# Norms of q computed one channel per partition and spread over the partitions by a diagonal product; first transposes ahead of the norms; four groups beside the first softmax

## The chip, the cores and the metric

The kernel runs on one core of one Trainium2 chip. The metric is device time in microseconds (us) of one execution; lower is better. Engines are named as the profile names them: PE is TensorE (matrix products; PEld is the loading of its weights), DVE is VectorE, ACT is ScalarE, POOL is GpSimd, SP is SyncE, which here only issues loads. Each engine works through its own instructions in order; they wait for each other on semaphores.

## What is computed

Attention over channels, with its product fused into a gated convolution. q, k, v are (4, 6336, 256), all in fp32:

```python
qn = q / (np.linalg.norm(q, axis=1, keepdims=True) + 1e-06)
kn = k / (np.linalg.norm(k, axis=1, keepdims=True) + 1e-06)
s = kn.transpose(0, 2, 1) @ qn / tau          # 256 x 256 for each of 4 batches
s = s - s.max(-1, keepdims=True)
a = np.exp(s)
a /= a.sum(-1, keepdims=True) + 1e-09
x = v @ a                                     # (4, 6336, 256)
# causal depthwise convolution over 5 rows, a gate, and two 256 x 256 products
gate = 1 / (1 + np.exp(-sum(conv_w[k] * shifted(x, k) for k in range(5))))
out = (gate * (x @ w_val)) @ w_out
```

The kernel does not normalise q and k ahead of the product. It sums k'q over the 6336 rows, sums the squares of every column of q and k beside it, and divides the 256 x 256 result once.

## The kernel before

**Groups.** A batch's rows are cut into 49 blocks of 128 rows and a rest of 64, and the blocks into 17 *groups*: the first has one block and the rest, the other 16 have three blocks. `load_group` loads a group of q and k (SP's queue). `score_group` squares it on ACT (`sq`, L209; the first block of a batch straight into the sums, L205), adds the squares on DVE (`acc_ps`, L214) and POOL (`acc`, L214), and returns the products that add k'q into the PSUM tile `s_ps` (L226). A block is multiplied either as it is (`raw`, one plain fp32 product for each half of k's channels) or split: ACT rounds it to fp32r (`hi`, L192), POOL subtracts to get the remainder (`lo`, L193), and three fp32r products stand for one. Which, is in one line: batch 0 multiplies most blocks raw, batch 1 its first LEAD groups, all else is split.

```python
nw, nv = (GROUP, 1 if g else 2) if b == 1 and g < LEAD else (0, 2)   # nw blocks raw, nv added on DVE
```

**Softmax.** `softmax(b)` is a generator that is advanced one stage by each `tick()`: `acc_all`, the sum of the two sums of squares (DVE L240), and a copy of `s_ps` to SBUF (ACT L242), which frees `s_ps` for the next batch; the norms (PE L245, L247) into a PSUM bank `n_ps`; Sqrt (ACT L252); on DVE the added epsilon (L256), two reciprocals (L257, L258), the scores scaled by both norms (L263) and their row minimum (L265); Exp (ACT L268); the sum's reciprocal and the scaled matrix `a` (L272, L275); `w`, its split into hi and lo (L278, L279); its transposes (PE L285, ACT `at` L289); and its product with w_val (PE L294, split by L298 and L299). So `x = v a` and the value product both read v alone, with two weights. `s_ps` and `acc_ps` exist once; the other PSUM tiles named here share four banks (`tag="bank"`), of which the norms hold one until L272.

In L245 the squares of q are summed over the partitions by a 128 x 128 matrix of ones, so that every partition gets all 256 norms of q along its row; the norms of k come out one channel per partition (L247), which is how the rows of the scores need them.

**Steps.** The rows of v are cut into 13 *steps* of 508 rows for each batch, 52 in all. For each, `transpose_v` (PE L335, ACT L336 `v_hi`, DVE L337 `v_lo`), `conv` (12 products L345 into `x_ps`, ACT L359, 8 DVE operations L361), `sigmoid` (ACT L367), `value` (12 products L345 into `val_ps`, DVE L374), `split_g` (ACT L387, POOL L388) and `finish` (24 products L404 into `o_ps`, ACT L414, stores from ACT's queue).

**Order.** The program starts with the 17 groups of batch 0, then a stretch written out by hand in which batch 1's first LEAD groups stand beside the softmax of batch 0, and then a loop over the 52 steps, in which the remaining groups are spread:

```python
due = NG + LEAD + -(-(total - NG - LEAD) * (n + 1) // (last + 1))
turns = min(due, total) - (issued - len(ready))
```

with NG = 17, total = 68 and last = 35. `turns` groups are multiplied in step n, the first near its start and the second, where there is one, near its end; their rounding, squares and subtraction are issued one group ahead. The four softmaxes' stages are advanced by the ticks of the steps that follow a batch's last group. A scheduler then orders each engine's instructions by its own estimate of times, with three means to steer it: `tc.high_priority()`, program order, and `behind(...)`, which keeps what is issued in it behind the marked instruction of an engine (`marks["PE"]`, `marks["ACT"]`).

Of the kernel before, what the change touches and what calls it, by code (L numbers as in the profile page):

```python
# [8 lines left out]
F32 = mybir.dt.float32  # L9
# [3 lines left out]
AF = mybir.ActivationFunctionType  # L13
# [3 lines left out]

P = 128
GROUP = 3
LEAD = 5  # L20
PREFETCH = 4
VLEAD = 2
SIDE = 11
# [5 lines left out]
def kernel(  # L29
# [136 lines left out]
    def score_group(b, g):  # L166
# [49 lines left out]
        def mms(np_, j):  # L216
            r = slice(0, np_)
            stop = g == NG - 1 and np_ == parts[-1][0] and j == parts[-1][1] + parts[-1][2] - 1
            for h in range(NH):
                hs = slice(h * P, (h + 1) * P)  # L220
                if j < nw:
                    ops = [(raw[r, j, 1, hs], raw[r, j, 0, :])]
                else:
                    ops = [(hi[r, j, 1, x, hs], hi[r, j, 0, y, :]) for x, y in ((0, 0), (0, 1), (1, 0))]
                for n_, (lhs, rhs) in enumerate(ops):
                    nc.tensor.matmul(st["s"][:, h, :], lhs, rhs, start=False,  # L226
                                     stop=stop and h == NH - 1 and n_ == len(ops) - 1)

        def clear():

# [5 lines left out]
    def softmax(b):  # L236
# [2 lines left out]
        acc = soft_p.tile([P, 2, C], F32, name="acc_all")  # L239
        nc.vector.tensor_tensor(acc, st["acc"], st["side"], ALU.add)  # L240
        s = soft_p.tile([P, NH, C], F32, name="s")
        nc.scalar.copy(s, st["s"])  # L242
        yield
        n_ps = ps.tile([P, 512], F32, name="o_ps", tag="bank")
        nc.tensor.matmul(n_ps[:, 0:C], ones, acc[:, 0, :], start=True, stop=True)  # L245
        for h in range(NH):
            marks["PE"] = nc.tensor.matmul(n_ps[:, C + h:C + h + 1], acc[:, 1, h * P:(h + 1) * P], ones[:, 0:1],  # L247
                                           start=True, stop=True)
        yield

        r, rk, z = n_ps[:, 0:C], n_ps[:, C:C + NH], n_ps[:, C + NH:C + 2 * NH]
        marks["ACT"] = nc.scalar.activation(n_ps[:, 0:C + NH], n_ps[:, 0:C + NH], AF.Sqrt)  # L252
        if b == 0:
            marks["ACT"] = tc.keep_in_program_order(nc.scalar.activation(dummy, dummy, AF.Exp))
        yield
        nc.vector.tensor_scalar(n_ps[:, 0:C + NH], n_ps[:, 0:C + NH], 1e-6, None, ALU.add)  # L256
        nc.vector.reciprocal(rk, rk)  # L257
        nc.vector.reciprocal(r, r)  # L258
        nk = soft_p.tile([P, NH], F32, name="nk")
        nc.vector.tensor_scalar(nk, rk, rtau, -1.0, ALU.mult, ALU.mult)  # L260

        for h in range(NH):
            nc.vector.scalar_tensor_tensor(s[:, h, :], s[:, h, :], nk[:, h:h + 1], r, ALU.mult, ALU.mult)  # L263
        m = soft_p.tile([P, NH], F32, name="m")
        nc.vector.tensor_reduce(m, s, axis=AX.X, op=ALU.min)  # L265
        yield
        for h in range(NH):
            marks["ACT"] = nc.scalar.activation(s[:, h, :], s[:, h, :], AF.Exp, scale=-1.0, bias=m[:, h:h + 1], accum_out=z[:, h:h + 1])  # L268
# [57 lines left out]
    def transpose_v(b, i, h):  # L326
# [5 lines left out]
        tp = ps.tile([P, 512], F32, name="t_ps", tag="bank")  # L332
        for j in range(-(-w // P)):
            np_ = min(P, w - j * P)
            nc.tensor.transpose(tp[:, j * P:j * P + np_], src[0:np_, j, h * P:(h + 1) * P], ident[0:np_, 0:np_])  # L335
        nc.scalar.copy(th[:, h, 0:w], tp[:, 0:w])  # L336
        nc.vector.tensor_tensor(tl[:, h, 0:w], tp[:, 0:w], th[:, h, 0:w].bitcast(F32), ALU.subtract)  # L337

# [114 lines left out]
    def run_group():  # L453
        if not ready:
            split_group()
        if not ready:
            return
        b, g, products = ready.pop(0)
        for f in products:
            f()  # L460
        if g == NG - 1:
            stages.append(softmax(b))
            if b:
                tick()
# [30 lines left out]
        for _ in gen:  # L495
            pass
    prep.clear()
    run_group()
    tick()
    tick()  # L500
    tick()
    with behind("PE", "ACT"):
        run_group()
        for h in range(NH):
            transpose_v(*step(0), h)
    tick()
    tick()
    with behind("ACT"):
# [1 line left out]
    tick()  # L510
    tick()
    tick()
    with behind("ACT"):
        for n in range(3, LEAD):
            run_group()
    for h in range(NH):
        conv(*step(0), h)
    while stages:
# [77 lines left out]
```

## Time and profile before

| | |
|---|---|
| time, median of 3 runs | 656.65 us (656.63 to 656.83) |
| the profiled execution's own time | 658.18 us |
| its span, first to last instruction | 656.3 us |
| PE busy | 637.8 us, 97% |
| DVE, ACT, POOL busy | 80%, 71%, 55% |
| TensorE's granted clock, mean | 0.996 |

The profile is of one execution. Busy time of PE is counted with modelled ends, so the time between the starts of two products says more of a product's price than its own length. Where an instruction waited, its row ends in brackets: the idle time of its engine just before it and what ended that.

### The profile page before, as it was taken

What the parts mean: (1) busy time and instruction counts of PE and PEld (TensorE: products, weight loads), DVE (VectorE), ACT (ScalarE), POOL (GpSimd) and SP (SyncE); (2) the same over time, 40 slices, a digit from 0 to 9 for tenths busy, and PEclk for the clock granted to TensorE, in tenths of its full rate; (3) what the DMA queues carried; (4) which work ended last, traced back from release to release, by engine and by line L of the source; (5) the groups of instructions that cost most, each with busy time, mean ns of one, the idle gap of its engine ahead of it and who ended that gap; (6) DMA issues with size and microseconds to landing.
All of it is one profiled execution on the core that took longest, in us unless ns stands there. A gap on an engine that the chain in (4) does not pass through costs nothing.

```text
span 656.3 us, 10656 instructions
## 1 busy us (share of the span) xinstructions
PE 637.8 (97%) x4008; PEld 571.1 (87%) x4008; DVE 523.0 (80%) x832; ACT 466.1 (71%) x607; POOL 360.8 (55%) x173
## 2 busy tenths in 40 slices
PE   7989999999999999999998999999999999999996
PEld 5868799989979999999997998998999798888886
DVE  3898689787878688778788688778778888888894
ACT  4565978867888768668698687767777756655564
POOL 2442796965837769659565497766763222312220
PEclk9999999999999999999999999999999999999999
DMA  8999874555635565545564365563222343443213
GB/s 268 322 328 337 267 225 152 161 166 165 179 103 176 188 195 176 173 132 170 175 184 121 109 217 158 189 185 104 65 78 71 118 126 95 121 129 104 65 50 100
DMA packets 107875, 105.75 MB, mean 161 GB/s; under 512 B 5744, under 2 KB 107312, under 8 KB 107824
## 3 DMA queue, kind: packets, MB, share of 16 engines
q1 hardware_dynamic: 81520, 79.24, 39.0%
q10 hardware_dynamic: 26304, 25.84, 13.9%
q8 instruction: 31, 0.51, 0.3%
q14 instruction: 20, 0.16, 0.1%
HBM read 79.11 MB, written 25.95 MB: 160 GB/s over the span
## 4 chain that ended last, share of the span: by engine, by line
PE 85%; ACT 5%; DVE 4%; POOL 2%; DMA 2%; issue 1%; SPq 1%; ACTq 0%; POOLq 0%
PE o_ps L404 20%; PE x_ps L345 20%; PE val_ps L345 19%; PE s_ps L226 18%; PE t_ps L335 6%; POOL hi L193 1%; ACT sq L209 1%; PE o_ps L294 1%; DMA raw<-in_k_dram 1%; DVE acc_ps L214 1%; ACT hi L192 1%; DVE gate L361 1%; DMA v_raw<-in_v_dram 1%; DVE gate L374 1%; ACT gate L367 0%
## 5 line engine op out<-in xcount | busy, mean ns | idle before, releaser
L361 DVE SCALAR_TENSOR_TENSOR gate<-x_ps,wa,gate 128x508 f32<-128x508 f32 (+1 forms) x416 | 275.4, 716 | 15.7 <-ACT gate L359 14.6
L193 POOL TENSOR_TENSOR hi<-raw,hi 128x1536 fp32r<-128x1536 f32 (+2 forms) x54 | 167.8, 3110 | 94.5 <-ACT hi L192 94.5
L388 POOL TENSOR_TENSOR g_lo<-gate,g_hi 128x1016 fp32r<-128x1016 f32 (+1 forms) x50 | 116.6, 2332 | 145.2 <-ACT g_hi L387 130.6
L214 DVE TENSOR_TENSOR acc_ps<-acc_ps,sq 128x512 f32<-128x512 f32 (+1 forms) x134 | 93.4, 697 | 74.8 <-ACT sq L209 71.6
L345 PE MATMUL x_ps<-v_hi,w 128*128 128x512 f32 (+1 forms) x416 | 139.1, 394 | 0.0
L345 PE MATMUL val_ps<-v_hi,w 128*128 128x508 f32 (+1 forms) x416 | 133.9, 383 | 0.8 <-ACT o_sb L414 0.7
L226 PE MATMUL s_ps<-hi 128*128 128x256 f32 (+1 forms) x852 | 121.1, 287 | 7.4 <-ACT hi L192 4.0
L226 PEld LDWEIGHTS s_ps<-hi 128*128 128x128 f32 (+1 forms) x852 | 110.7, 190 | 13.9 <-ACT hi L192 5.5
L404 PE MATMUL o_ps<-wo_hi,g_hi 128*128 128x256 f32 x400 | 113.2, 283 | 1.7 <-ACT g_hi L383 1.5
L414 ACT COPY o_sb<-o_ps 128x512 f32<-128x512 f32 x99 | 58.2, 589 | 79.1 <-PE o_ps L404 77.9
L404 PE MATMUL o_ps<-wo_lo,g_hi 128*128 128x256 f32 x400 | 112.1, 280 | 0.0
L404 PE MATMUL o_ps<-wo_hi,g_lo 128*128 128x256 f32 x400 | 111.7, 280 | 0.0
L209 ACT ACTIVATE sq<-raw 128x1536 f32<-128x1536 f32 (+3 forms) x69 | 96.0, 1393 | 16.5 <-DVE acc_ps L214 7.9
L214 POOL TENSOR_TENSOR acc<-acc,sq 128x512 f32<-128x512 f32 x58 | 76.4, 1318 | 39.7 <-ACT sq L209 39.3
L345 PEld LDWEIGHTS x_ps<-v_hi,w 128*128 128x128 f32 x416 | 78.2, 190 | 14.3 <-DVE gate L361 0.2
L345 PEld LDWEIGHTS val_ps<-v_hi,w 128*128 128x128 f32 x416 | 77.1, 188 | 14.5 <-ACT o_sb L414 0.9
L359 ACT ACTIVATE gate<-x_ps,wa 128x508 f32<-128x508 f32 (+1 forms) x104 | 68.2, 671 | 20.5 <-PE x_ps L345 20.2
L336 ACT CAST v_hi<-t_ps 128x512 fp32r<-128x512 f32 (+1 forms) x104 | 55.8, 569 | 36.2 <-PE t_ps L335 36.2
L345 PE MATMUL x_ps<-v_lo,w 128*128 128x512 f32 (+1 forms) x208 | 80.2, 386 | 0.0
L345 PE MATMUL val_ps<-v_lo,w 128*128 128x508 f32 (+1 forms) x208 | 79.2, 381 | 0.0
L374 DVE TENSOR_TENSOR gate<-val_ps,gate 128x508 f32<-128x508 f32 (+1 forms) x104 | 64.3, 657 | 18.3 <-ACT gate L367 14.0
L404 PEld LDWEIGHTS o_ps<-wo_hi,g_hi 128*128 128x128 f32 x400 | 75.2, 188 | 3.1 <-ACT g_hi L383 1.7
(84 smaller groups left out, 799.3 us busy)
## 6 DMA issues: line engine op xcount, KB each, us to landing
raw<-in_q_dram SPq DMA_DIRECT2D x64, 384.0 KB
raw<-in_k_dram SPq DMA_DIRECT2D x64, 384.0 KB
v_raw<-in_v_dram SPq DMA_DIRECT2D x44, 512.0 KB
out_dram<-o_sb ACTq DMA_DIRECT2D x48, 384.0 KB
out_dram<-o_sb ACTq DMA_DIRECT2D x48, 124.0 KB
v_raw<-in_v_dram SPq DMA_DIRECT2D x4, 384.0 KB
raw<-in_q_dram SPq DMA_DIRECT2D x4, 128.0 KB
raw<-in_k_dram SPq DMA_DIRECT2D x4, 128.0 KB
```

The costliest lines, as they stand in the source:

```text
L193: nc.gpsimd.tensor_tensor(hi[r, js, :, 1, :], raw[r, js, :, :], hi[r, js, :, 0, :].bitcast(F32), ALU.subtract)
L209: nc.scalar.activation(sq[0:np_, ja:jb], raw[0:np_, ja:jb], AF.Square)
L214: eng.tensor_tensor(st[key][0:np_], st[key][0:np_], sq[0:np_, j], ALU.add)
L226: nc.tensor.matmul(st["s"][:, h, :], lhs, rhs, start=False, stop=stop and h == NH - 1 and n_ == len(ops) - 1)
L336: nc.scalar.copy(th[:, h, 0:w], tp[:, 0:w])
L345: nc.tensor.matmul(ps, wt[:, which, ws, ch, hs], vs[:, ch, lo:hi_], start=n_ == 0, stop=n_ == 3 * NH - 1)
L359: nc.scalar.activation(gate[:, h, 0:w], x_ps[:, 0:w], AF.Copy, scale=cw[:, h, 0:1])
L361: nc.vector.scalar_tensor_tensor(gate[:, h, 0:w], x_ps[:, tap:tap + w], cw[:, h, tap:tap + 1], gate[:, h, 0:w], ALU.mult, ALU.add)
L374: nc.vector.tensor_tensor(gate[:, h, 0:w], val_ps[:, 0:w], gate[:, h, 0:w], ALU.mult)
L388: nc.gpsimd.tensor_tensor(gl[:, :, 0:w], gate[:, :, 0:w], gh[:, :, 0:w].bitcast(F32), ALU.subtract)
L404: nc.tensor.matmul(o_ps[:, u * C:(u + 1) * C], gs[:, h, off:off + P], ws[:, h, :], start=n_ == 0, stop=n_ == 3 * NH - 1)
L414: marks["ACT"] = nc.scalar.copy(o_sb[:, j:j + len(pair), :], o_ps[:, 0:len(pair) * C].rearrange("p (j c) -> p j c", c=C))
```

## The change

Six things change.

1. **Norms.** L245's product with the full matrix of ones goes. The squares of q are summed like those of k, one channel per partition: four products of one column (new L248) in place of one of 256 columns and two of one. Sqrt, the epsilon and the reciprocals then work on 4 columns (or 2) in place of 258 and 256.
2. **Spreading.** The two columns of 1/norm(q) are turned into two diagonal matrices by ACT (new L265, `diag`, identity scaled per partition), and two plain fp32 products of ones with them (new L269) write the 256 values to every partition, into the same PSUM bank. The scores' scaling L263 (new L272) reads them there.
3. **First transposes.** `transpose_v` of step 0 stands ahead of the norms, with high priority, behind the last score product and the copy of `s_ps`; before, it stood behind batch 1's first two groups. Batch 1's first group comes behind it and the norms.
4. **LEAD is 4**, so four groups of batch 1 stand beside the first softmax, not five. The fifth is multiplied in the loop, and split, not raw.
5. Since LEAD stands in `due`, the remaining 47 groups (before: 46) fall otherwise on the steps. Batch 1's last group falls in step 9 (before: 8), batch 2's in step 22 (before: 21), batch 3's in step 35 as before; in steps 9 and 22 the next batch's first group follows in the same step.
6. The other edits are marks that `behind` uses.

```diff
-LEAD = 5
+LEAD = 4
@@ softmax
-        nc.scalar.copy(s, st["s"])
+        marks["ACT"] = nc.scalar.copy(s, st["s"])
         yield
         n_ps = ps.tile([P, 512], F32, name="o_ps", tag="bank")
-        nc.tensor.matmul(n_ps[:, 0:C], ones, acc[:, 0, :], start=True, stop=True)
-        for h in range(NH):
-            marks["PE"] = nc.tensor.matmul(n_ps[:, C + h:C + h + 1], acc[:, 1, h * P:(h + 1) * P], ones[:, 0:1],
-                                           start=True, stop=True)
+        for x in range(2):
+            for h in range(NH):
+                marks["PE"] = nc.tensor.matmul(n_ps[:, x * NH + h:x * NH + h + 1], acc[:, x, h * P:(h + 1) * P], ones[:, 0:1],
+                                               start=True, stop=True)
         yield
-        r, rk, z = n_ps[:, 0:C], n_ps[:, C:C + NH], n_ps[:, C + NH:C + 2 * NH]
-        marks["ACT"] = nc.scalar.activation(n_ps[:, 0:C + NH], n_ps[:, 0:C + NH], AF.Sqrt)
+        norm, rk, z = n_ps[:, 0:2 * NH], n_ps[:, NH:2 * NH], n_ps[:, 2 * NH:3 * NH]
+        r = n_ps[:, P:P + C]
+        marks["ACT"] = nc.scalar.activation(norm, norm, AF.Sqrt)
+        yield
+        nc.vector.tensor_scalar(norm, norm, 1e-6, None, ALU.add)
+        rq = soft_p.tile([P, NH], F32, name="rq")
+        nc.vector.reciprocal(rq, n_ps[:, 0:NH])
+        nc.vector.reciprocal(rk, rk)
+        nk = soft_p.tile([P, NH], F32, name="nk")
+        nc.vector.tensor_scalar(nk, rk, rtau, -1.0, ALU.mult, ALU.mult)
+        diag = soft_p.tile([P, NH, P], F32, name="diag")
+        for h in range(NH):
+            marks["ACT"] = nc.scalar.activation(diag[:, h, :], ident, AF.Copy, scale=rq[:, h:h + 1])
         if b == 0:
             marks["ACT"] = tc.keep_in_program_order(nc.scalar.activation(dummy, dummy, AF.Exp))
-        yield
-        nc.vector.tensor_scalar(n_ps[:, 0:C + NH], n_ps[:, 0:C + NH], 1e-6, None, ALU.add)
-        nc.vector.reciprocal(rk, rk)
-        nc.vector.reciprocal(r, r)
-        nk = soft_p.tile([P, NH], F32, name="nk")
-        nc.vector.tensor_scalar(nk, rk, rtau, -1.0, ALU.mult, ALU.mult)
+        for h in range(NH):
+            marks["R"] = nc.tensor.matmul(r[:, h * P:(h + 1) * P], ones, diag[:, h, :], start=True, stop=True)
@@ after batch 0's groups
-    run_group()
     tick()
-    tick()
-    tick()
+    with tc.high_priority(), behind("PE", "ACT"):
+        for h in range(NH):
+            transpose_v(*step(0), h)
+    with behind("PE"):
+        tick()
     with behind("PE", "ACT"):
         run_group()
-        for h in range(NH):
-            transpose_v(*step(0), h)
     tick()
     tick()
     with behind("ACT"):
@@
-    with behind("ACT"):
-        for n in range(3, LEAD):
+    with behind("R", "ACT"):
+        for n in range(2, LEAD):
             run_group()
+    tick()
```

What the built program makes of it stands below; these are orders, without times. First PE around the first softmax, from batch 0's last score products (`s_ps<-hi`) to the first convolution's first product (`x_ps`). `t_ps` are the transposes of step 0, `o_ps<-...acc_all` the norms, `s_ps<-zeros` the product that clears `s_ps`, `o_ps<-ident,a` the transposes of the softmax's result. Before:

```order
L226 MATMUL s_ps<-hi 128x256 x6
L231 MATMUL s_ps<-zeros 128x512
L226 MATMUL s_ps<-raw 128x256 x4
L245 MATMUL o_ps<-acc_all,ones 128x256
L247 MATMUL o_ps<-ones,acc_all 128x1 x2
L226 MATMUL s_ps<-raw 128x256 x6
L335 MATMUL t_ps<-ident,v_raw 128x128 x8
L226 MATMUL s_ps<-raw 128x256 x18
L285 MATMUL o_ps<-ident,a 128x128 x4
L345 MATMUL x_ps<-v_hi,w 128x512
```

The same stretch of PE in the changed program:

```order
L226 MATMUL s_ps<-hi 128x256 x6
L344 MATMUL t_ps<-ident,v_raw 128x128 x8
L248 MATMUL o_ps<-ones,acc_all 128x1 x4
L231 MATMUL s_ps<-zeros 128x512
L226 MATMUL s_ps<-raw 128x256 x10
L269 MATMUL o_ps<-diag,ones 128x128 x2
L226 MATMUL s_ps<-raw 128x256 x12
L294 MATMUL o_ps<-ident,a 128x128 x4
L354 MATMUL x_ps<-v_hi,w 128x512
```

The transposes and all norms now stand ahead of the clearing and of every product of batch 1, the two diagonal products stand behind ten of the raw products, and six raw products are gone.

Second, ACT around the second softmax (batch 1's), from the stores of a finished step. L252 and L254 are its Sqrt, L242 the copy of the scores, L192 the rounding of the next batch's first and second group, L367 and L376 the sigmoid of the running step. Before:

```order
L192 CAST hi<-raw 128x2x256
L192 CAST hi<-raw 64x2x256
L209 ACTIVATE sq<-raw 64x512
L418 DMA out_dram<-o_sb 128x3x256
L420 DMA out_dram<-o_sb 124x256
L205 ACTIVATE acc_ps<-raw 128x512
L242 COPY s<-s_ps 128x512
L252 ACT_TABLE_LOAD
L252 ACTIVATE o_ps<-o_ps 128x258
L367 ACT_TABLE_LOAD
L367 ACTIVATE gate<-gate 128x1016
L336 CAST v_hi<-t_ps 128x512
```

The same place of ACT in the changed program:

```order
L254 ACT_TABLE_LOAD
L254 ACTIVATE o_ps<-o_ps 128x4
L429 DMA out_dram<-o_sb 124x256
L242 COPY s<-s_ps 128x512
L192 CAST hi<-raw 128x2x256
L192 CAST hi<-raw 64x2x256
L205 ACTIVATE acc_ps<-raw 128x512
L209 ACTIVATE sq<-raw 64x512
L376 ACT_TABLE_LOAD
L376 ACTIVATE gate<-gate 128x1016
L265 ACTIVATE diag<-ident,rq 128x128 x2
L192 CAST hi<-raw 128x6x256
```

The rounding of the first group moved from ahead of Sqrt to behind it, and the rounding of the second group (128x6x256), which before stood behind the softmax's Exp, follows the diagonals.

Third, PE of the changed program at the same softmax: its diagonal products, between the products of the next batch's first group. Twelve products of `finish` (`o_ps<-wo...`, of which the first three are shown) and then, in one row, the 18 of the second group come behind these:

```order
L226 MATMUL s_ps<-hi 128x256 x11
L269 MATMUL o_ps<-diag,ones 128x128 x2
L226 MATMUL s_ps<-hi 128x256
L344 MATMUL t_ps<-ident,v_raw 128x128 x4
L413 MATMUL o_ps<-wo_hi,g_hi 128x256
L413 MATMUL o_ps<-wo_lo,g_hi 128x256
L413 MATMUL o_ps<-wo_hi,g_lo 128x256
```

Before, none of the diagonal products was there, and the second group's products stood behind a whole `finish`, a `value` and a `conv`. The third softmax has the same order as the second in the changed program, on both engines.

## Rows read from the trace of the kernel before

**Rows 1.** The page's part 1: engine, busy us (share of span), instructions.

```profile
PE 637.8 (97%) x4008; PEld 571.1 (87%) x4008; DVE 523.0 (80%) x832; ACT 466.1 (71%) x607; POOL 360.8 (55%) x173
```

**Rows 2.** Windows: stretch, its length, busy PE PEld DVE ACT POOL, PEclk, DMA share, GB/s.

```profile
175.00:206.00 31.00, 30.21 (x179) 25.73 (x179) 25.42 (x43) 27.49 (x39) 14.06 (x7) 1.00 0.47 136
206.00:336.00 130.00, 130.00 (x872) 119.14 (x871) 102.61 (x164) 97.61 (x122) 94.18 (x42) 1.00 0.56 170
336.00:372.00 36.00, 33.31 (x212) 30.06 (x211) 30.12 (x51) 28.97 (x42) 17.71 (x9) 0.95 0.51 151
497.00:526.00 29.00, 27.75 (x167) 23.90 (x165) 24.07 (x42) 21.84 (x34) 5.41 (x3) 1.00 0.31 90
```

**Rows 3.** Timeline, first softmax, PE and DVE: start us, us, engine, line, operation, count, [idle before].

```profile
55.77 0.50 PE L231 MATMUL s_ps<-zeros 128*128 128x512 f32 x1 [0.68 <-ACT s L242]
56.18 0.69 DVE L240 TENSOR_TENSOR acc_all<-acc_ps,acc 128x512 f32<-128x512 f32 x1
...
62.56 7.94 PE L226 MATMUL s_ps<-raw 128*128 128x256 f32 x36
...
73.66 1.99 PE L294 MATMUL o_ps<-wa,at 128*128 128x256 f32 x8
...
81.30 2.41 PE L226 MATMUL s_ps<-hi 128*128 128x256 f32 x18 [0.52 <-POOL hi L193]
```

**Rows 4.** Timeline, second softmax, PE: the longer of its two waits.

```profile
194.43 2.30 PE L226 MATMUL s_ps<-hi 128*128 128x256 f32 x17 [0.45 <-POOL hi L193]
```

**Rows 5.** Timeline (PE) and windows: an early wait; the third softmax's wait.

```profile
40.15 0.86 PE L226 MATMUL s_ps<-hi 128*128 128x256 f32 x5 [1.44 <-POOL hi L193]
...
40.00:44.00 4.00, 2.97 (x14) 2.21 (x14) 3.85 (x6) 2.12 (x3) 0.95 (x2) 1.00 1.10 348
...
357.86 0.53 PE L226 MATMUL s_ps<-hi 128*128 128x256 f32 x1 [2.69 <-ACT hi L192]
...
358.00:362.00 4.00, 4.00 (x12) 3.19 (x13) 1.72 (x3) 3.97 (x5) 4.00 (x2) 0.58 0.32 79
```

**Rows 6.** Timeline, fourth softmax, PE: from its norms on.

```profile
498.80 0.59 PE L245 MATMUL o_ps<-acc_all,ones 128*128 128x256 f32 x2
499.23 0.50 PE L247 MATMUL o_ps<-ones,acc_all 128*128 128x1 f32 x4
499.59 1.08 PE L226 MATMUL s_ps<-hi 128*128 128x256 f32 x7
...
503.25 0.60 PE L335 MATMUL t_ps<-ident,v_raw 128*128 128x128 f32 x4
503.61 0.48 PE L345 MATMUL x_ps<-v_hi,w 128*128 128x512 f32 x1
...
506.46 0.60 PE L335 MATMUL t_ps<-ident,v_raw 128*128 128x128 f32 x4
...
510.57 0.50 PE L345 MATMUL val_ps<-v_hi,w 128*128 128x508 f32 x1 [0.68 <-ACT o_sb L414]
```

**Rows 7.** Timeline, fourth softmax, ACT: Sqrt, the scores' copy and the sigmoid.

```profile
500.08 1.28 ACT L252 ACT_TABLE_LOAD   x1 [0.50 <-DVE gate L361]
...
501.38 0.37 ACT L252 ACTIVATE o_ps<-o_ps 128x258 f32<-128x258 f32 x1
501.66 0.59 ACT L242 COPY s<-s_ps 128x512 f32<-128x512 f32 x1
...
503.56 1.05 ACT L367 ACTIVATE gate<-gate 128x1016 f32<-128x1016 f32 x1
```

**Rows 8.** Groups by line and shape: shapes, count | busy us, mean ns | idle before.

```profile
L193 POOL TENSOR_TENSOR hi<-raw,hi 128x1536 fp32r<-128x1536 f32 x44 | 154.8, 3520 | 88.3 <-ACT hi L192 88.3
...
L192 ACT CAST hi<-raw 128x1536 fp32r<-128x1536 f32 x44 | 65.0, 1479 | 0.0
...
L258 DVE RECIPROCAL o_ps<-o_ps 128x256 f32<-128x256 f32 x4 | 7.1, 1763 | 0.1
...
L275 ACT ACTIVATE a<-s,rz 128x256 f32<-128x256 f32 x8 | 3.6, 498 | 1.9 <-DVE rz L272 1.9
```

More of the change, by code (lines that the diff above doesn't have):

```diff
@@ L225, in mms @@
                 for n_, (lhs, rhs) in enumerate(ops):
-                    nc.tensor.matmul(st["s"][:, h, :], lhs, rhs, start=False,
-                                     stop=stop and h == NH - 1 and n_ == len(ops) - 1)
+                    marks["PE"] = nc.tensor.matmul(st["s"][:, h, :], lhs, rhs, start=False,
+                                                   stop=stop and h == NH - 1 and n_ == len(ops) - 1)
         def clear():
@@ L241, in softmax @@
         s = soft_p.tile([P, NH, C], F32, name="s")
-        nc.scalar.copy(s, st["s"])
+        marks["ACT"] = nc.scalar.copy(s, st["s"])
         yield
         n_ps = ps.tile([P, 512], F32, name="o_ps", tag="bank")
-        nc.tensor.matmul(n_ps[:, 0:C], ones, acc[:, 0, :], start=True, stop=True)
-        for h in range(NH):
-            marks["PE"] = nc.tensor.matmul(n_ps[:, C + h:C + h + 1], acc[:, 1, h * P:(h + 1) * P], ones[:, 0:1],
-                                           start=True, stop=True)
-        yield
-        r, rk, z = n_ps[:, 0:C], n_ps[:, C:C + NH], n_ps[:, C + NH:C + 2 * NH]
-        marks["ACT"] = nc.scalar.activation(n_ps[:, 0:C + NH], n_ps[:, 0:C + NH], AF.Sqrt)
+        for x in range(2):
[6 more added lines that the diff above has]
+        marks["ACT"] = nc.scalar.activation(norm, norm, AF.Sqrt)
+        yield
+        nc.vector.tensor_scalar(norm, norm, 1e-6, None, ALU.add)
[5 more added lines that the diff above has]
+        diag = soft_p.tile([P, NH, P], F32, name="diag")
+        for h in range(NH):
+            marks["ACT"] = nc.scalar.activation(diag[:, h, :], ident, AF.Copy, scale=rq[:, h:h + 1])
         if b == 0:
             marks["ACT"] = tc.keep_in_program_order(nc.scalar.activation(dummy, dummy, AF.Exp))
-        yield
-        nc.vector.tensor_scalar(n_ps[:, 0:C + NH], n_ps[:, 0:C + NH], 1e-6, None, ALU.add)
-        nc.vector.reciprocal(rk, rk)
-        nc.vector.reciprocal(r, r)
-        nk = soft_p.tile([P, NH], F32, name="nk")
-        nc.vector.tensor_scalar(nk, rk, rtau, -1.0, ALU.mult, ALU.mult)
+        for h in range(NH):
+            marks["R"] = nc.tensor.matmul(r[:, h * P:(h + 1) * P], ones, diag[:, h, :], start=True, stop=True)
         for h in range(NH):
@@ L264, in softmax @@
         m = soft_p.tile([P, NH], F32, name="m")
-        nc.vector.tensor_reduce(m, s, axis=AX.X, op=ALU.min)
+        marks["DVE"] = nc.vector.tensor_reduce(m, s, axis=AX.X, op=ALU.min)
         yield
@@ L334, in transpose_v @@
             np_ = min(P, w - j * P)
-            nc.tensor.transpose(tp[:, j * P:j * P + np_], src[0:np_, j, h * P:(h + 1) * P], ident[0:np_, 0:np_])
+            marks["PE"] = nc.tensor.transpose(tp[:, j * P:j * P + np_], src[0:np_, j, h * P:(h + 1) * P], ident[0:np_, 0:np_])
         nc.scalar.copy(th[:, h, 0:w], tp[:, 0:w])
```

## The prediction

> **What bounds the kernel now.** I read the busy times first: PE is busy 637.8 of 656.3 us [rows 1]. Then windows, to see where the rest lies. A stretch of the loop without a softmax has no idle time on PE at all, 130.00 of 130.00 us [rows 2], so that there only the number and price of PE's products can change the end. Idle time lies beside the softmaxes: 0.79 us in the window of the second, 2.69 of the third, 1.25 of the fourth [rows 2]. The timeline then says what ended it. At the first softmax PE waits 0.68 us for the copy of the scores, and 0.52 us for POOL's remainder of the fifth group [rows 3]. At the second it waits 0.45 us for POOL [rows 4]. At the third it is one wait, 2.69 us for ACT's rounding of the next batch's first group, and behind it TensorE ran at 0.58 of its clock for four microseconds [rows 5], between its two levels of 1.2 and 2.4 GHz; since at half speed work takes twice as long, 4.0 x (1 - 0.58) = 1.7 us went there. A wait of 1.44 us had left the clock at 1.00 [rows 5]. So the point from which a wait costs clock too lies between 1.44 and 2.69 us here.
>
> **PE's own work, each softmax.** Before, the norms took 0.79 us, from 498.80 to 499.59: 0.43 for the wide product and 0.18 for each narrow one [rows 6]. Now they are four narrow ones, 0.72. The diagonal products are new: two plain fp32 products of 128 columns. No row has one. Above, each is bounded by a raw one of 256 columns, 7.94 / 18 = 0.44 us [rows 3], below by a transpose of 128 columns, (503.61 - 503.25) / 4 = 0.09 [rows 6]. I take half a raw one, 0.22, since it is the same operation with half the columns: 0.43 for both. PE's net is 0.72 + 0.43 - 0.79 = **+0.36** per softmax, between +0.1 and +0.8.
>
> **First softmax.** The last score product ended at 55.77 - 0.68 = 55.09, and the sum of the squares at 56.18 + 0.69 = 56.87 [rows 3]. The eight transposes now fill 55.09 to 55.8 (8 x 0.09), and then PE waits for that sum, until about 56.95: 1.1 us where it waited 0.68. From there by order: norms 0.72, the clearing 0.33, 22 raw products 22 x 0.44 = 9.8 (some a little shorter, having 64 rows), diagonals 0.43, transposes of the result 0.36, the products x 2.85 (503.61 to 506.46 in [rows 6]). The product with w_val (L294, `aw`) then starts at about 71.45, where it started at 73.66: **-2.2**. This is six raw products (2.6) less the longer wait and the diagonals. The chain behind `aw` is unchanged: its split by ACT, then that of the next group by ACT and POOL, up to the 18 products at 81.30; these stood 7.64 us behind `aw`, and I put them at 79.1. The fifth group, now in the loop, adds 18 split products there: 18 x 0.12 = 2.2 (2.30 us for 17 by [rows 4], modelled ends included). Sum of the first softmax: **0.0**. It rests on the softmax's own chain being done before PE wants its result. By the durations of before, the scaled scores would be ready at about 64.2 and `w` split at 68.6, for PE's 69.1: half a microsecond to spare, and each microsecond more of that chain is one on the end. DVE has less to do there, since the reciprocal of 256 columns was 1.76 us [rows 8].
>
> **Second softmax.** Here ACT's order decides. PE's work from the norms' start N on is by order: norms 0.72, 7 products of the first group 0.92 (the rest between 499.59 and 503.25, 2.74, being `value`), 2.74, transposes 0.36, x 2.85 [rows 6], clearing 0.33, 12 more products 1.5, diagonals 0.43, transposes 0.36, 12 of `finish` 1.5. So PE asks for the second group's remainder about N + 11.7. POOL gets there like this: ACT's table load starts at N + 1.28 and Sqrt at N + 2.58, as in [rows 7]; Sqrt on 4 columns ends at 2.8; the copy 3.3; four operations of up to 512 columns, now between Sqrt and the sigmoid, at 0.5 each (the copy's price less overlap) 5.4; a table load 6.7; the sigmoid 1.05, to 7.75 [rows 7]; two diagonals; the rounding 1.48; POOL's subtraction 3.52 [rows 8]. A diagonal lies between nothing and the 0.50 of an ACT operation on 256 columns (L275, [rows 8]); at 0.25 each, POOL ends at 7.75 + 0.5 + 1.48 + 3.52 = N + 13.25. **PE waits 1.5 us for POOL, 13 us behind the norms**, and about 0.3 more for the result's transposes. Before, the window's idle time was 0.79 [rows 2]. Sum: 1.8 - 0.79 + 0.36 = **+1.35**.
>
> The Trainium skill, page "ScalarE: Activation LUTs", section "What ACT_TABLE_LOAD costs", speaks against this order more strongly: a switch of tables is said to cost a drain of about 1380 ns beside the load of 1283 ns. The trace does not agree here: the load took 1.28 us and Sqrt started 0.02 us behind it [rows 7].
>
> **Third softmax.** It has the order of the second now. The wait of 2.69 goes, and with it the 1.7 of clock; in come the 1.8 of the same wait on POOL and 0.36 of work: 1.8 + 0.36 - 2.69 - 1.7 = **-2.2**.
>
> **Fourth softmax.** No next batch's group stands there. The 0.68 us for which `value` waited on the copy of `finish` [rows 6] should go, since in the new order that copy stands ahead of Exp's table load. Against that, the row minimum, in DVE's new order behind more of the running step's work, comes later, and so may the result. I set 0.3 for that: -0.68 + 0.36 + 0.3 = **0.0**, from -0.4 to +0.4.
>
> **Elsewhere.** The remaining groups fall otherwise on the steps, but a stretch without idle time costs its products wherever they stand. Added ACT and DVE operations beside them are hidden by PE: ACT is busy 97.61 of 130 us [rows 2]. Without that cover the diagonals on ACT would be 4 x 0.5 = 2 us at most.
>
> **Sum.** 0.0 + 1.35 - 2.2 + 0.0 = -0.85, rounded to -0.9: from the profiled 658.18 us to 657.3. That execution was 1.53 us above the median of 656.65, and I take the same offset: **655.7 us**. A difference of about 0.2%, 1.3 us, is the least that can be told from no change, so faster means below 655.3 and slower above 658.0; 655.7 is just inside "same". Own range of this case: from 654.4 (the transposes' price for the diagonals, and a wait at the second softmax shorter by the diagonals' 0.5) to 656.9 (the upper price).
>
> **The rivals.**
> *No wait on POOL.* If the scheduler's order runs on the chip such that ACT's rounding comes 1.5 us sooner or PE 1.5 us later, both waits at the second and third softmax go: 655.7 - 2 x 1.5 = **652.7**. For it: many small terms on PE's side, of which each makes PE later; the loop's other rounding of this shape is hidden by 206 to 336 without any wait [rows 2]. Against it: ACT's chain has one more diagonal pair and four operations more ahead of the sigmoid, and POOL's 3.52 us can't shrink.
> *The waits only move.* Each softmax keeps the idle time that it had, the third its 2.69 with the clock, because a later group of the same chain is late in place of the first. Then only PE's work remains at the second and third, 2 x 0.36 = 0.7: 656.65 + 0.7 = **657.4**; should the second lose its 1.35 beside that, 658.4. For it: PE there wants 18 products from ACT and POOL that come no sooner than in the second. Against it: the wait was for ACT's rounding, which now stands 4 us ahead of its place.
> *The clock falls twice (slower).* If ACT's chain at the second and third softmax is 1.2 us later than I have it, the wait of 1.5 is 2.7, and from there the clock falls as in [rows 5]. Each then costs 1.2 + 1.7 = 2.9 more: **661.5** for both, 658.6 for one. It decides from the point between 1.44 and 2.69 us. For it: the summed ACT chain has ten links, and PE's wait at the third softmax was of that size. Against it: the wait has to grow by 0.8 of itself.
> *Each table load has a drain.* Two switches stand in that chain, so that it ends 2 x 1.4 later, the wait is 4.3 and each softmax costs 2.8 + 1.7 more: 655.7 + 9 = **664.7**. That is the page's rule above, and the 0.02 us of [rows 7] are against it.
>
> **How the numbers follow.** The forecast has 0.48, of which 0.20 lies below 655.3 and 0.28 in "same". No wait on POOL 0.20, all faster. The waits only move 0.15, of which 0.12 same and 0.03 slower. The clock falls 0.14, all slower. A drain 0.01. What no case names, 0.02, slower. So faster 0.40, same 0.40, slower 0.20. The range goes from 652.4, a little below the faster rival, to 658.7, where the clock falls at one softmax; below it I leave about 0.08 and above it 0.10.
>
> **What would show it.** In the changed kernel's timeline: PE's norms at about 56.9 behind a wait of 1.1 us on DVE, and x of the first step without a wait; at the second and third softmax a wait of some 1.5 us on POOL about 13 us behind the norms, none on ACT's rounding of the first group, and no window with a clock near half; the diagonals at 0.2 us each. The window of the third softmax should show idle time of 1.8 for 2.69. The forecast is wrong if `w` is later than PE at the first softmax, since there nothing covers it, or if a wait passes the point at which the clock falls.

## The result: slower by 0.4%, with two kinds of executions

The changed kernel takes 660.15 us (median of 18 runs, 656.21 to 663.03), the kernel before 656.76 beside it. The ratio of the two sets of runs is 1.0040, with a 95% interval from 1.0025 to 1.0054 (the two medians alone give 1.0052). So the change is slower, and 660.15 lies above the prediction's range, which ended at 658.7. A second set of runs gave 1.0031 (1.0014 to 1.0048). Two executions of the experiments, of 2242.5 and 3604.78 us, are left out of the ratios and of the counts of executions below.

The executions of either kernel fall into two groups, which the mean granted clock tells apart. Beside four of the sets of runs, the kernel before was mostly near 656 us in 23 of 81 executions (clock 0.999) and mostly near 658 us in 58 (0.994 to 0.997). The changed kernel was near 657 us in 9 of 29 (0.998 or more) and mostly near 660 us in 20 (0.993 to 0.997); executions and traces without the loss of clock are called undisturbed below. The profile of before came from its slower group, that of after from its faster one.

The page of after, part 1, then the windows of [rows 2] (stretch, length, busy PE, PEld, DVE, ACT, POOL, PEclk, DMA share, GB/s):

```profile
PE 637.6 (97%) x4038; PEld 571.2 (87%) x4038; DVE 515.7 (79%) x833; ACT 468.7 (72%) x616; POOL 362.5 (55%) x173
...
175.00:206.00 31.00, 30.38 (x194) 26.74 (x192) 22.58 (x41) 26.96 (x41) 18.46 (x10) 1.00 0.52 148
206.00:336.00 130.00, 130.00 (x875) 119.35 (x875) 105.67 (x168) 99.35 (x124) 92.92 (x42) 1.00 0.57 172
336.00:372.00 36.00, 35.40 (x231) 31.68 (x231) 26.95 (x49) 29.57 (x46) 17.43 (x8) 1.00 0.49 145
497.00:526.00 29.00, 27.31 (x163) 23.14 (x162) 21.15 (x40) 22.74 (x38) 5.03 (x3) 1.00 0.30 91
```

The third softmax now has 0.60 us of idle time for 2.69 and no lost clock, the second 0.62 for 0.79, the fourth 1.69 for 1.25. Nothing here is a loss of 3 us. This execution's span is 654.9 us, less than the 656.3 of before.

Two executions can't be compared by the clock on the wall, since the stretch up to the end of batch 0 takes a little more or less each time: its last score product started at 54.81 us in the profile of before and at 53.71 in that of after. Counted from that product, the traces of one kernel agree within some 0.25 us, apart from stretches at half clock. The table gives, for the start of the same product in each trace, its distance from that product, less the same distance in the profile of before. The points are step 0's `value` (behind the first softmax), step 16's (behind the second), step 35's (behind the third) and the kernel's last product. With four groups beside the first softmax, PE has done 6 raw products (12 records) fewer up to step 16 than before, and by step 35 it has also done the 18 split ones that stand for them (870 records of split score products in the whole program, for 852).

```
trace             us      clock   step 0   step 16  step 35  last
before            658.18  0.996    0.00     0.00     0.00     0.00
before_second     657.24  0.996    0.00    -0.02    -0.18    -0.20
before_fifth      657.36  0.996   +0.01    +0.01    -0.23    -0.24
after             656.69  0.998   -2.02    -1.99    -2.12    -0.79
after_look        656.28  0.999   -2.03    -2.00    -2.15    -0.80
after_third       657.79  0.999   -2.01    -1.99    -2.14    -0.82
after_fourth      660.43  0.995   +1.26    +1.30    +1.14    +2.49
after_fifth       659.57  0.997   -0.39    -0.37    -0.52    +0.83
undo_lead         662.72  0.997   +0.51    +5.58    +3.40    +4.73
undo_norms        659.02  0.999   -1.91    -0.39    +0.92    +0.89
undo_first        661.57  0.994   +2.04    +2.08    +1.94    +3.29
lead4_alone       656.49  0.998   -1.07    -0.37    -1.25    -1.25
group_first       657.55  0.998   -1.84    -1.82    -1.97    -0.63
best3             655.16  0.998   -1.84    -1.82    -2.00    -1.97
best3_again       656.62  1.000   -1.83    -1.80    -1.95    -1.90
```

The three undisturbed traces of after agree to 0.03 us, at -0.8 for the whole. The two slower ones leave them ahead of step 0's `value` by 3.3 and 1.6 us, and run parallel from there. So the loss lies in the first softmax.

### The profile page after: what moved, and what is told of

It is laid out like the page before. It is cut to its first block, busy times and chain, and to the rows that moved or that the text cites. A ratio compares the mean times of both kernels' runs of the same rounds, so it can differ in the third digit from the quotient of the medians.

```text
span 654.9 us, 10744 instructions
## 1 busy us (share of the span) xinstructions
PE 637.6 (97%) x4038; PEld 571.2 (87%) x4038; DVE 515.7 (79%) x833; ACT 468.7 (72%) x616; POOL 362.5 (55%) x173
## 4 chain that ended last, share of the span: by engine, by line
PE 84%; ACT 5%; DVE 5%; POOL 2%; issue 1%; DMA 1%; SPq 1%; ACTq 0%; DVEq 0%
PE o_ps L413 21%; PE x_ps L354 20%; PE val_ps L354 19%; PE s_ps L226 16%; PE t_ps L344 6%; DVE acc_ps L214 3%; POOL hi L193 2%; ACT sq L209 1%; PE o_ps L303 1%; DMA raw<-in_k_dram 1%; ACT hi L192 1%; ACT L376 1%; SPq L74 0%; ACT o_sb L423 0%; PE o_ps L248 0%
## 5 line engine op out<-in xcount | busy, mean ns | idle before, releaser
L193 POOL TENSOR_TENSOR hi<-raw,hi 128x1536 fp32r<-128x1536 f32 (+2 forms) x55 | 171.5, 3121 | 109.4 <-ACT hi L192 109.4
L226 PE MATMUL s_ps<-hi 128*128 128x256 f32 (+1 forms) x870 | 124.2, 287 | 3.6 <-POOL hi L193 3.2
L226 PEld LDWEIGHTS s_ps<-hi 128*128 128x128 f32 (+1 forms) x870 | 113.1, 190 | 8.9 <-POOL hi L193 4.3
```

The source lines that it names most:

```text
L193: nc.gpsimd.tensor_tensor(hi[r, js, :, 1, :], raw[r, js, :, :], hi[r, js, :, 0, :].bitcast(F32), ALU.subtract)
L226: marks["PE"] = nc.tensor.matmul(st["s"][:, h, :], lhs, rhs, start=False, stop=stop and h == NH - 1 and n_ == len(ops) - 1)
```

## The experiments

**The changed kernel again (five more traces).** No edit.

> The changed kernel as it is, for a second trace. Its first trace, of an execution of 656.69 us, shows no stretch at half clock in any softmax; the median of its runs is 660.15 us. Theory C (the clock falls in most executions): an execution of 660 to 661 us shows a new stretch of 4 us or more near half clock right behind one of PE's waits beside a softmax, worth 1.7 us or more, and the wait ahead of it is longer than in the first trace (over 1.4 us). Theory W (a wait alone): the granted clock is 1.00 at all four softmaxes, and one wait is longer by 3.5 us.

> The changed kernel once more, for a third trace, with the same expectations: by theory C executions near 657 us have no stretch at half clock and those near 660.5 us have one, always at the same softmax; by theory W the clock never differs.

> The changed kernel for one more trace. Its executions so far fall into two groups, near 657 us with a mean granted clock of 0.998 to 0.999, and near 660.3 us with 0.995; both traces so far are of the first group. Theory C: a trace of the second group has one stretch near half clock behind a wait of PE of more than 1.4 us. By what the two traces have, the longest late wait is the fourth softmax's, 1.4 us for `at`, so I expect it there, near 517 us. Rival: at the second or third softmax, whose waits for POOL would then be 1.5 us or more in place of 0.8.

after_again gave the second ratio above; its trace is of the execution of 2242.5 us and says nothing of these groups. after_look (656.28 us) and after_third (657.79) have no stretch at half clock anywhere.

> The changed kernel for a further trace, to find an execution of about 660 us. The traces so far (three, all with a clock of 0.998 or more) have the same wait of 0.95 us ahead of the norms of the first softmax, and no stretch at half clock. The run with the first transposes moved back has a longer wait there, 1.85 us, and its clock was at 0.50 from about 58 to 64 us. Theory C, now with its place: an execution near 660 us has a stretch near half clock right behind that wait, from about 56 to 62 us, and nowhere else beside a softmax. Rival: it has it at the fourth softmax, behind the wait of 1.4 us for `at`.

> The changed kernel once more, with the same expectations: an execution near 660 us has its half clock behind the norms' wait of the first softmax (theory C), or behind the wait for `at` at the fourth (rival); one near 657 us has none at either place.

after_fourth took 660.43 us, after_fifth 659.57. First, PE beside the first softmax in the profile of after, undisturbed (start us, us, operation, count; in brackets the idle time before):

```profile
53.83 1.03 PE L344 MATMUL t_ps<-ident,v_raw 128*128 128x128 f32 x8
55.82 1.05 PE L248 MATMUL o_ps<-ones,acc_all 128*128 128x1 f32 x8 [0.95 <-DVE acc_all L240]
56.73 0.48 PE L231 MATMUL s_ps<-zeros 128*128 128x512 f32 x1
57.05 4.87 PE L226 MATMUL s_ps<-raw 128*128 128x256 f32 x20
61.76 0.61 PE L269 MATMUL o_ps<-diag,ones 128*128 128x128 f32 x4
...
67.38 0.60 PE L294 MATMUL o_ps<-ident,a 128*128 128x128 f32 x4
67.74 0.47 PE L354 MATMUL x_ps<-v_hi,w 128*128 128x512 f32 x1
...
70.57 1.97 PE L303 MATMUL o_ps<-wa,at 128*128 128x256 f32 x8
```

(Here a plain fp32 product leaves two records and a transpose one: x8 at the norms are four products, x20 are ten, x8 at the transposes are eight.) The same place in after_fourth, and its windows there:

```profile
56.26 1.05 PE L248 MATMUL o_ps<-ones,acc_all 128*128 128x1 f32 x8 [0.95 <-DVE acc_all L240]
57.17 0.48 PE L231 MATMUL s_ps<-zeros 128*128 128x512 f32 x1
57.49 8.15 PE L226 MATMUL s_ps<-raw 128*128 128x256 f32 x20
65.48 0.61 PE L269 MATMUL o_ps<-diag,ones 128*128 128x128 f32 x4
...
56.00:60.00 4.00, 3.74 (x15) 2.83 (x16) 2.63 (x8) 2.86 (x7) 0.00 (x0) 0.71 1.10 351
60.00:64.00 4.00, 4.00 (x10) 2.72 (x10) 0.70 (x1) 2.06 (x5) 1.26 (x1) 0.50 1.09 347
64.00:68.00 4.00, 4.00 (x21) 3.55 (x20) 1.56 (x3) 0.19 (x1) 0.00 (x0) 0.93 1.09 346
```

Same instructions, same wait of 0.95 us. Behind it the ten raw products take from 57.49 to 65.48, 7.99 us, where they took 61.76 - 57.05 = 4.71: **3.3 us**, and the clock is at 0.50 in the window between, its level of 1.2 GHz. after_fifth has a shorter stretch (0.60 from 60 to 64 us), worth 1.6. Theory C holds, at the first softmax; the rival at the fourth falls, since the traces run parallel there.

The Trainium skill, page "TensorE: Matmul & The Clock Gate", section "Part 1: The HAM clock gate (the "warmup" mystery)", says that the chip watches TensorE's activity in windows that run freely, not from the kernel's start, and that transitions so vary from run to run. This fits a wait of one and the same length that costs clock in some executions and none in others; no run here shows such windows.

**The wait ahead of the norms, longer.** The first transposes behind the norms and batch 1's first group:

```diff
-    with tc.high_priority(), behind("PE", "ACT"):
-        for h in range(NH):
-            transpose_v(*step(0), h)
     with behind("PE"):
         tick()
     with behind("PE", "ACT"):
         run_group()
+        for h in range(NH):
+            transpose_v(*step(0), h)
```

> The changed kernel with the transposes of step 0 behind batch 1's first group, where they stood behind the norms. By my sum the early transposes hide 0.7 us of PE's work under the wait for the sum of the squares, so undoing this costs 0.3 to 0.7 us at the first softmax and changes nothing at the others: about 660.5 for the median. If it is faster than the changed kernel, the early transposes cost something that I did not see.

661.13 us, ratio 1.0055 (1.0034 to 1.0077); six of seven executions have 0.997 or less. Norms and a window in its trace:

```profile
56.60 1.05 PE L248 MATMUL o_ps<-ones,acc_all 128*128 128x1 f32 x8 [1.85 <-DVE acc_all L240]
...
60.00:64.00 4.00, 4.00 (x14) 3.07 (x14) 1.30 (x2) 2.99 (x7) 1.27 (x1) 0.50 1.09 348
```

The longer wait brought the half clock in nearly every execution, and here no transposes stand ahead of it. Of the change's parts the early transposes help: with the half clock in both, 3.29 - 2.49 = 0.8 us by the table, for my 0.3 to 0.7.

**No wait ahead of the norms.** Batch 1's first group ahead of them; PE's order is transposes, clearing, 4 raw products, norms, 6 raw products, diagonals:

```diff
+    run_group()
     with behind("PE"):
         tick()
-    with behind("PE", "ACT"):
-        run_group()
     tick()
     tick()
-    with behind("ACT"):
+    with behind("PE", "ACT"):
         run_group()
```

> The changed kernel with batch 1's first group ahead of the norms: PE's order is transposes, clearing, 4 raw products, norms, 6 raw products, diagonals. The wait of 0.95 us goes, since the sum of the squares is there when PE gets to the norms; all behind is the same. Theory C at the first softmax: every execution has a mean clock of 0.998 or more, none is at 0.995, and the median is 1 us below the undisturbed executions of the changed kernel, about 656 to 656.5, some 4 us below its median. Rival (the fourth softmax): more than a third of the executions still have 0.995, and the median is about 659.

657.35 us, ratio 1.0003 (0.9991 to 1.0015), and 11 of 12 executions have a clock of 0.998 or more. So the half clock is gone with the wait, as theory C says. The edit does two things at once, though: it fills the wait, and it puts raw products between the transposes and the norms. Which of the two keeps the clock up isn't separated here. And the undisturbed time is no shorter. Its PE, timeline:

```profile
57.72 1.05 PE L248 MATMUL o_ps<-ones,acc_all 128*128 128x1 f32 x8
...
67.14 0.84 PE L294 MATMUL o_ps<-ident,a 128*128 128x128 f32 x4
68.19 0.50 PE L354 MATMUL x_ps<-v_hi,w 128*128 128x512 f32 x1 [0.21 <-ACT w L287]
...
71.42 1.99 PE L303 MATMUL o_ps<-wa,at 128*128 128x256 f32 x8 [0.21 <-ACT at L298]
```

The wait has moved to the end of the softmax: PE now waits for `w` and `at`, because the chain norms, Sqrt, diagonals, Exp, `w` starts later. From the start of the result's transposes to that of x it is 1.05 us for 0.36 in after, and `at`'s products start 3.23 us behind x for 2.83: together 1.1 us, as much as the wait that went. So my 1 us for it was wrong. The wait ahead of the norms itself cost nothing that was not due anyway; its price was the clock behind it.

**LEAD = 5 in the changed kernel.**

```diff
-LEAD = 4
+LEAD = 5
```

> The changed kernel with LEAD = 5 again: five groups beside the first softmax, and batch 1's last group in step 8, batch 2's in step 21, as before the change. Theory C with the place at the second or third softmax: the order of the running step and the norms there is as it was, so the time is that of the kernel before within 0.5 us or up to 2 us better. Theory C with the place at the first softmax (its shorter cover): also gone, since 18 more raw products stand there. If the loss is at the fourth softmax, where the groups fall as before in both, nothing is gained: about 660.

663.98 us, ratio 1.0118 (1.0089 to 1.0148): none of the three. The table has +5.1 us at the second softmax. PE and ACT there, and a window:

```profile
199.57 0.69 PE L294 MATMUL o_ps<-ident,a 128*128 128x128 f32 x2 [3.42 <-ACT a L284]
...
195.17 1.28 ACT L277 ACT_TABLE_LOAD   x1
...
200.00:204.00 4.00, 4.00 (x24) 3.85 (x22) 4.00 (x7) 1.83 (x4) 1.59 (x1) 0.63 0.24 22
```

In this order the sigmoid stands between the two Exps, each with a table load, so that `a` is 3.42 us late, and there the clock falls as well. The new norms don't stand alone: they need the steps on which LEAD = 4 puts the groups.

**The old norms in the changed kernel.** The product with ones and the reciprocals of before, without diagonals:

```diff
-        for x in range(2):
-            for h in range(NH):
-                marks["PE"] = nc.tensor.matmul(n_ps[:, x * NH + h:x * NH + h + 1], acc[:, x, h * P:(h + 1) * P], ones[:, 0:1],
+        nc.tensor.matmul(n_ps[:, 0:C], ones, acc[:, 0, :], start=True, stop=True)
...
-            marks["ACT"] = nc.scalar.activation(diag[:, h, :], ident, AF.Copy, scale=rq[:, h:h + 1])
...
+        nc.vector.reciprocal(r, r)
...
-            marks["R"] = nc.tensor.matmul(r[:, h * P:(h + 1) * P], ones, diag[:, h, :], start=True, stop=True)
```

> The changed kernel with the norms of q by the wide product of ones, without diagonals: DVE's two reciprocals of 258 and 256 columns come back, four groups and early transposes stay. If the loss hangs on the new form of the norms (the added step PE, ACT, PE ahead of the scaled scores), this gives 656 to 657 us; if it hangs on the four groups and the steps on which the rest falls, it stays at about 660.

658.78 us, ratio 1.0019 (1.0006 to 1.0032). Between the two answers that I had set: 9 of 12 executions are without loss of clock, though the wait ahead of the norms is 0.96 us, but they are near 658.7. By the table the second softmax takes +1.5 us where the new form takes 0.0, and the third +1.3 where it takes -0.1. At the fourth it is the other way: 0.0 for +1.3. So the new form is worth 1.6 us in all at full clock, and the clock that it lost more often is its price. Why the same wait ahead of the wide product cost clock so seldom (3 of 12, none of them traced) stays open.

**LEAD = 4 in the kernel before.**

```diff
-LEAD = 5
+LEAD = 4
```

> The kernel before with four groups beside the first softmax and nothing else changed. If the loss comes from the groups that fall otherwise on the steps (batch 1's last in step 9, batch 2's in step 22), this is slower than before by 1.5 us or more, and its second and third softmaxes wait for POOL as in the changed kernel. If it comes from the new norms, it is within 1 us of before, and the third softmax no longer waits 2.7 us for ACT's rounding.

656.35 us, ratio 0.9985 (0.9973 to 0.9996): slightly faster than before. All 12 executions have 0.998 or more. Its third softmax:

```profile
336.00:372.00 36.00, 35.20 (x229) 31.66 (x228) 30.03 (x50) 32.01 (x46) 19.61 (x11) 1.00 0.58 170
```

0.8 us idle for 2.69, at full clock. So the third softmax's wait goes by the steps on which the groups fall, and the new norms aren't needed for that; nor do those steps bring the changed kernel's loss.

**The kernel before again (five more traces).**

> The kernel before for a second trace. Its executions also fall into two groups, near 655.7 us with a clock of 0.999 and near 657.8 with 0.996 to 0.997; the trace that the prediction rests on, 658.18 us at 0.996, belongs to the second. Theory B (the baseline): an execution near 655.7 us shows the third softmax without the stretch at half clock, with PE's wait there still above 2 us or shorter, and all else alike within 0.5 us. Then 1.7 us of my saving of 2.2 at the third softmax was to be had in only part of the executions.

> The kernel before for a further trace. Theory B: an execution near 655.8 us has no stretch near half clock behind the third softmax's wait at 356 to 358 us, while the wait itself is as in the other traces, 2.7 us, and all products stand as far from batch 0's last score product as there, within 0.1 us up to that wait and about 1.7 to 1.9 us nearer behind it. Rival: its wait is shorter by 1 us or more, so that the two groups differ by a wait and the clock only follows. An execution near 657.8 us has the half clock as the two traces so far.

> The kernel before once more, with the same expectations: near 655.8 us no half clock at the third softmax and the same wait of 2.7 us (theory B), or a shorter wait (rival); near 657.8 us the half clock behind the wait.

> The kernel before for one more trace. Theory B: an execution near 655.8 us has the wait of 2.7 us at the third softmax and no stretch near half clock behind it; one near 657.8 us has both. Rival: the faster one's wait is shorter by 1 us or more.

> As for the other look at the kernel before: near 655.8 us the wait of 2.7 us without half clock (theory B) or a wait shorter by 1 us (rival), near 657.8 us the wait and the half clock.

They took 657.24, 657.61, 657.62, 657.36 and 658.09 us, all with a clock of 0.996 and the half clock at the third softmax. That of before_third:

```profile
357.42 0.58 PE L226 MATMUL s_ps<-hi 128*128 128x256 f32 x1 [2.69 <-ACT hi L192]
...
356.00:360.00 4.00, 2.58 (x7) 2.10 (x8) 3.06 (x6) 3.98 (x5) 2.50 (x1) 0.65 0.44 122
```

All six traces of the kernel before are of its slower group. That the faster group's 2 us are the same half clock left out is an inference from the mean clock of 0.999; whether its wait is shorter stays open.

**A version from both.** group_first, with the changed kernel's norms and diagonals for batches 0 to 2 and the norms of before for batch 3:

```diff
+        if b < 3:
...
+        else:
...
+            nc.tensor.matmul(n_ps[:, 0:C], ones, acc[:, 0, :], start=True, stop=True)
...
+            nc.vector.reciprocal(r, r)
```

> As group_first, and the fourth softmax with the norms of q by the wide product, as before the change. By the distance of the same products in the traces, the fourth softmax of the changed kernel costs 1.3 us more than that of before, behind a wait of 1.4 us for `at`; with the old form there this goes. About 655, 1.2 us below group_first, and clearly faster than before. If the cost at the fourth softmax hangs on the order of the steps and not on the form of the norms, it is as group_first.

> The version with batch 1's first group ahead of the norms and the old norms at the fourth softmax, timed again beside the kernel before. Its products end 2.0 us nearer to batch 0's last score product than in the kernel before with the half clock at the third softmax, and about level with the kernel before without it. With two thirds of the executions of before at half clock there, the median should be 1.2 to 1.6 us below, a ratio of 0.9978 to 0.9985. If the explanation lacks a further loss, the ratio is 1.0 or above.

656.44 us, ratio 0.9987 (0.9973 to 1.0001), and again 656.18, 0.9973 (0.9959 to 0.9987): faster than the changed kernel, and than the kernel before by 0.1 to 0.3%, which the second interval shows and the first, since it takes in 1.0, does not. LEAD = 4 alone, one edit of one line, had 0.9985; the traces put best3 0.7 us ahead of it, the times don't tell them apart. 20 of 23 executions have 0.998 or more. Two of the other three took 655.71 and 656.19 us, no longer than the rest, so the mean clock alone says neither where clock was lost nor what it cost. The fourth softmax is what it was before, 29.00 - 27.75 = 1.25 us idle:

```profile
497.00:526.00 29.00, 27.75 (x168) 23.96 (x168) 23.71 (x43) 23.14 (x38) 5.85 (x3) 1.00 0.32 94
```

## Why the prediction was wrong

**The step that failed** is in its first paragraph: "A wait of 1.44 us had left the clock at 1.00. So the point from which a wait costs clock too lies between 1.44 and 2.69 us here." From one wait that cost nothing I made a safe length for all. At the first softmax, whose sum had no term for the clock, a wait of 0.95 us, which I had forecast (1.1), was followed by half clock worth 3.3 and 1.6 us in two of five traces, and by their mean clock 20 of 29 executions lost some. The wait of 1.44 stood between products of scores; this one stands between eight transposes ahead of it and four one-column products and the clearing behind it, so that from 53.83 to 57.05 us PE did nothing else. Whether that is the difference isn't shown: what the chip counts there these runs don't tell, and the wide norms with the same wait lost clock less often. The prediction's slower rival had the mechanism, but put it at the second and third softmax, where the clock stayed.

**The sum itself**, for undisturbed executions: -0.85 forecast, -0.79 measured. That is luck: its terms were wrong by -1.3 at the second softmax and +1.3 at the fourth. From the table, with the fifth group's 18 products, which are done by step 35, set at the first softmax as in the forecast (18 x 0.12 = 2.16):

- First softmax: -2.02 + 2.16 = +0.1, forecast 0.0. `aw` came 2.0 us earlier, forecast 2.2; the terms that I named for it (six raw products less the longer wait and the diagonals, 2.6 - 0.4 - 0.4) make only 1.8. My 69.1 for PE at x did not follow from my sum either, which has x at 71.45 - 2.85 = 68.6 and so nothing to spare. In after, `w` was there 0.5 us ahead of x, at 67.25, and x did not wait.
- Second: 0.0, forecast +1.35. The chain of ACT and POOL was right to 0.1: norms at 182.51, and

```profile
185.09 0.16 ACT L254 ACTIVATE o_ps<-o_ps 128x4 f32<-128x4 f32 x1
...
187.21 0.62 ACT L209 ACTIVATE sq<-raw 64x512 f32<-64x512 f32 x1
187.84 1.28 ACT L376 ACT_TABLE_LOAD   x1
189.14 1.05 ACT L376 ACTIVATE gate<-gate 128x1016 f32<-128x1016 f32 x1
190.10 0.68 ACT L265 ACTIVATE diag<-ident,rq 128x128 f32<-128x128 f32 x2
...
192.22 3.49 POOL L193 TENSOR_TENSOR hi<-raw,hi 128x1536 fp32r<-128x1536 f32 x1 [3.35 <-ACT hi L192]
...
192.00 0.71 PE L269 MATMUL o_ps<-diag,ones 128*128 128x128 f32 x4
...
195.76 1.45 PE L226 MATMUL s_ps<-hi 128*128 128x256 f32 x10 [0.62 <-POOL hi L193]
```

  POOL ended at 195.71, N + 13.2, as forecast (13.25). But PE got there 0.8 us later than my 11.7: the diagonals took 0.64 us here, not 0.43 (0.44 at the first softmax, 61.76 to 62.20), the norms 0.81, not 0.72, and the last product of the first group, with 64 rows, 0.31. The wait was 0.62, not 1.5, and the 0.3 for the transposes did not come. It is the rival "No wait on POOL" for half its way. Small terms on PE that I had called bounds of the cost were cover for the wait. With what was measured, 0.62 of wait for 0.79 and 0.81 + 0.64 of products for 0.79, my sum would be +0.5, where the table has 0.0; that difference is not accounted for.
- Third: -2.12 + 1.99 - 2.16 = -2.3, forecast -2.2. The long wait went, and lead4_alone shows that the steps on which the groups fall did this. But the wait that came in was 0.60, not 1.8, and with it and 0.66 of added products (0.81 + 0.64 - 0.79, as at the second) the same sum gives 0.60 + 0.66 - 2.69 - 1.7 = -3.1; the other 0.8 is not accounted for, so this term too came out by luck.
- Fourth: +1.35, forecast 0.0. PE and ACT in after:

```profile
512.90 0.89 ACT L284 ACTIVATE a<-s,rz 128x256 f32<-128x256 f32 x2
...
516.78 0.61 ACT L298 COPY at<-o_ps 128x512 f32<-128x512 f32 x1
...
517.45 0.38 PE L413 MATMUL o_ps<-wo_hi,g_hi 128*128 128x256 f32 x1 [1.39 <-ACT at L298]
```

  The 0.68 at `value` did go, as forecast. In its place `finish` waits 1.39 us for the copy of `at`, which stands behind ACT's `w`, two `v_hi` and `g_hi`, and by the kernel's text frees the bank that `finish` needs. I had read the order up to the result and not who else wanted its bank. best3 settles it: the old form there gives the 1.3 back.

**Table loads.** Here too Sqrt stands directly behind its load, 183.79 + 1.28 = 185.07 and 185.09, and the sigmoid's load at 187.84 stands 0.01 us behind the operation ahead of it and 0.02 ahead of the sigmoid. The drain that the Trainium skill's page "ScalarE: Activation LUTs", section "What ACT_TABLE_LOAD costs", adds to a switch of tables does not show on either side of that load. The rival with a drain falls.

```profile
183.79 1.28 ACT L254 ACT_TABLE_LOAD   x1 [0.50 <-DVE gate L370]
```

**The baseline.** I took a constant offset of 1.53 us between the profile and the median of three. It is not constant: the profile was of the group with lost clock, where by their mean clock 58 of 81 executions are, and in its own case the clock was lost at the third softmax. Of the 2.3 that the third softmax gave, 1.7 can be had in such executions alone. This would have moved the forecast up by half a microsecond. The measured median lies 4.45 us above the 655.7. The four undisturbed ones of its 18 executions have a median of 656.79, so 3.4 us of that are the loss of clock, which both slow traces have at the first softmax; of the other 1.1 the half microsecond is one part, and the rest is not accounted for.

## What to carry to other kernels

Of a wait that a change makes longer or moves, price the clock behind it too, and don't take one wait that cost no clock as a safe length for others: here the wait of 0.95 us cost nothing itself, and the products behind it took 3.3 or 1.6 us longer where the clock fell. Compare traces from a common product behind the loads, not from the span's start; the changed kernel's own first trace looked like a gain. And look at the granted clock of all executions of both kernels before taking one profile as the baseline.

## What the runs showed of the hardware that I had not expected

The same program with the same wait of 0.95 us ran into half clock in two of five traces and not in the other three, and then lost 3.3 or 1.6 us. Without half clock the traces of one kernel repeat closely over the 600 us behind batch 0's last score product: three of the changed kernel within 0.03 us, two of best3 within 0.07.

Two plain fp32 products of 128 columns took 0.44 us at the first softmax and 0.64 at the second, where 192.00 to 192.64 lies between split products.
